# Local and down-sampled attention feeding a feed-forward layer on one core: leaner softmax steps for the first two batches, one long pass over the last eight weight chunks, and wide idle products tied to the chain

## The chip, the core and the metric

The kernel runs on one core of one Trainium2 chip. The core has a matrix engine (PE, whose weight loads are listed as PEld), a vector engine (DVE), a scalar engine (ACT), a GpSimd engine (POOL) and a queue engine (SP) that issues most of the transfers. Each engine takes its instructions strictly in the order in which the program was written for it and waits on semaphores for the others. The metric is device time in microseconds (us) of a whole execution, lower is better.

## The reference, cut to what matters

There are 8 batches, 8 heads, 576 positions and a head width of 64. Each head's attention is the sum of two softmax attentions; all heads side by side then form the rows of a feed-forward layer.

```python
q_d = q.reshape(B, H, Sd, factor, D).mean(axis=3)      # factor 4, Sd = 144; k_d, v_d likewise
out_d = sm_attn(q_d, k_d, v_d)                         # full softmax over 144 positions
out_up = np.repeat(out_d, factor, axis=2)
mask = np.abs(pos[:, None] - pos[None, :]) < factor    # band of 7 positions
scores = np.where(mask, scale * (q @ k.T), -1e9)
out_local = softmax(scores) @ v
x = (out_up + out_local)                               # -> 4608 rows of 512
h = x @ w_in                                           # 512 x 2048
g = h * np.cos(h)
return g @ w_out                                       # 2048 x 512
```

## The kernel before, in words

**Attention units.** A unit is a pair of heads of one batch, four to a batch. Its steps are `u_qk` (load q and k, add each four neighbouring columns: line 490 on DVE, or lines 483 and 485 on POOL), `u_v` (load v twice: `vdn` for the down-sampled part, `vl` for the band), `u_s` (products of scores on PE, the softmax on DVE, ACT and POOL), `u_t` (transpose the probabilities, line 632 on DVE and line 648 on PE) and `u_pv` (probabilities by values on PE, lines 665 and 677, their sum on DVE at line 696, and the split of the result into x's high and low part, lines 711 and 399). Batches 0 and 1 (`b < NEARLY`) come before and between the first feed-forward steps; their tiles lie in the memory that later holds weight chunks 8 to 15, so in the profile they carry names such as `wxi` and `wxo`, and `xxl`. `sml` and `smd` are the scores of the band and of the down-sampled part, `su` the sums, `mxl` and `mxd` the maxima, `ptl` and `ptd` the transposed probabilities, `xs` the unit's output. A unit below is called (batch, pair), as in (1,0).

**Feed-forward.** The 4608 rows are 12 tiles of 384, the inner width 16 chunks of 128. One step is a tile by a chunk: `gemm1` (line 739, 12 products), then cosine work on ACT and DVE (lines 748 to 757), then two steps later `gemm2` (line 775, 9 products into three banks). Weights come as 64-bit words and are split into a high and a low part by lines 420 to 432 and 399 (`xxh` is their scratch; the input and the output matrix give two such splits for a chunk). `PASSES` sets the steps' order: tiles 0 to 2 take chunks in four groups of four, so each of these tiles is summed up in the output by four passes, each evacuated (line 791) and written; from tile 3 on one pass takes all 16 chunks.

**What sets the order.** `Plan` keeps every step as an operation with an estimated duration, and `schedule()` lays them out by list scheduling in the planner's own time; each engine's program is then written in that order. An operation with alternatives (`alts`) goes to the engine that would end it sooner. The first 40 loads are chained: each waits until the third one before it has landed (`AHEAD`), so a load's issue in the trace marks that landing. On PE, gaps of the plan are filled with wide idle products of an identity (line 892, `ident_b`, 128x512, result unused); ahead of each `u_s`, `u_t` and `u_pv` step of batch 0 stand at least two of them (`warm=2`).

## Time and profile before

| | us |
|---|---|
| median of 3 runs (lowest, highest) | 1010.02 (1004.89, 1184.49) |
| profiled execution, its time | 1007.4 |
| profiled execution, span first to last instruction | 1005.6 |
| PE busy | 981.2 (98%) |
| DVE busy | 681.7 (68%) |
| ACT busy | 610.2 (61%) |
| POOL busy | 221.3 (22%) |
| the chain that ended last: share of PE | 87% |

The span of the profiled execution is 1.8 us shorter than its time. Rows of a time line give the start, the busy time, the engine, the line and the operation, the tile written and the tiles read, the shape and the count. Busy times of neighbours overlap a little, since an instruction starts before the one ahead has wholly left the engine. The tables of windows give busy time (and count) for PE, PEld, DVE, ACT and POOL, then the granted clock of PE as a share of the full one, the share of the 16 DMA engines and GB/s.

### The profile page before, as it was taken

How to read it: one execution, taken by the hardware profiler on the slowest of the kernel's cores; microseconds unless marked ns; L12 is line 12 of the kernel's file. 1: busy time of each engine (PE TensorE's matmuls, PEld its weight loads, DVE VectorE, ACT ScalarE, POOL GpSimd, SP SyncE). 2: the span in 40 equal slices, each digit the busy share in tenths (PEclk: the TensorE clock that was granted, in tenths of full speed). 3: DMA queues.
4: the chain of work that ended last, by engine and by line, in shares of the span. 5: the costliest groups of instructions: out<-in, count | busy, mean ns of one | idle time of the engine just before them, and what ended most of it. 6: DMA issues, size and time to landing. Idle time of an engine off the chain costs nothing.

```text
span 1005.6 us, 23855 instructions
## 1 busy us (share of the span) xinstructions
PE 981.2 (98%) x9917; PEld 847.3 (84%) x9917; DVE 681.7 (68%) x1362; ACT 610.2 (61%) x1174; POOL 221.3 (22%) x280
## 2 busy tenths in 40 slices
PE   8878999999999999999999999999999999999998
PEld 4546899899887888889888888888888888899997
DVE  7799899986587578464758957655657865433433
ACT  3457588876576656555547746654646665655554
POOL 6775325631153202000002211200001300000000
PEclk9979799999999999999999999999999999999999
DMA  7784643424355322210212312201112320100000
GB/s 224 234 270 149 215 159 64 80 36 68 67 116 132 78 65 70 68 33 28 81 49 71 129 49 58 83 26 36 62 54 73 112 65 4 37 1 1 32 1 32
DMA packets 41051, 80.70 MB, mean 80 GB/s; under 512 B 4976, under 2 KB 16240, under 8 KB 40944
## 3 DMA queue, kind: packets, MB, share of 16 engines
q1 hardware_dynamic: 37056, 72.11, 23.2%
q0 software_dynamic: 3888, 7.08, 5.0%
q8 instruction: 78, 1.28, 0.5%
q14 instruction: 29, 0.24, 0.1%
HBM read 57.93 MB, written 16.52 MB: 74 GB/s over the span
## 4 chain that ended last, share of the span: by engine, by line
PE 87%; DVE 6%; DMA 4%; issue 1%; ACT 1%; SPq 0%; ACTq 0%; DVEq 0%
PE bank L775 38%; PE bank L739 38%; PE bank L539 2%; PE bank L684 2%; PE bank L555 2%; PE bank L665 2%; PE bank L648 1%; DMA q<-qT 1%; DMA wdi<-w_in 1%; PE bank L892 1%; PE bank L677 1%; DMA vl<-vl 1%; DVE su L609 1%; DMA wxi<-qT 0%; DVE wxo L615 0%
## 5 line engine op out<-in xcount | busy, mean ns | idle before, releaser
L775 PE MATMUL bank<-wo,gh 128*128 128x512 f32 x1152 | 363.5, 396 | 0.0
L775 PEld LDWEIGHTS bank<-wo,gh 128*128 128x128 f32 x1152 | 210.0, 188 | 38.0 <-issue 3.1
L775 PE MATMUL bank<-wo,gl 128*128 128x512 f32 x576 | 227.6, 396 | 0.0
L750 ACT ACTIVATE tr<-bank,bmagic 128x384 f32<-128x384 f32 x192 | 110.9, 577 | 113.5 <-PE bank L739 109.7
L754 DVE SCALAR_TENSOR_TENSOR tr<-tr,bank 128x384 f32<-128x384 f32 x192 | 105.0, 547 | 108.0 <-ACT tr L749 107.1
L751 DVE SCALAR_TENSOR_TENSOR tr<-tr,bank 128x384 f32<-128x384 f32 x192 | 105.6, 550 | 84.2 <-ACT tr L750 83.2
L748 ACT ACTIVATE tr<-tr 128x384 f32<-128x384 f32 x192 | 100.7, 524 | 77.0 <-DVE tr L751 76.4
L756 ACT ACTIVATE gh<-tr 128x384 fp32r<-128x384 f32 x163 | 85.3, 523 | 88.3 <-DVE tr L754 86.8
L399 DVE TENSOR_TENSOR gl<-tr,gh 128x384 fp32r<-128x384 f32 x154 | 92.4, 600 | 63.5 <-ACT gh L756 60.5
L775 PEld LDWEIGHTS bank<-wo,gl 128*128 128x128 f32 x576 | 108.0, 187 | 23.5
L739 PE MATMUL bank<-x0h,wi 128*128 128x384 f32 x384 | 107.5, 340 | 0.0
L739 PE MATMUL bank<-x1h,wi 128*128 128x384 f32 x384 | 107.1, 339 | 0.0
L739 PE MATMUL bank<-x2h,wi 128*128 128x384 f32 x384 | 106.8, 338 | 0.0
L739 PE MATMUL bank<-x3h,wi 128*128 128x384 f32 x384 | 106.5, 338 | 0.0
L749 ACT ACTIVATE tr<-tr 128x384 f32<-128x384 f32 x192 | 100.8, 525 | 6.1
L399 POOL TENSOR_TENSOR gl<-tr,gh 128x384 fp32r<-128x384 f32 x38 | 43.0, 1132 | 269.6 <-DVE gh L757 175.8
L739 PEld LDWEIGHTS bank<-x0h,wi 128*128 128x128 f32 x384 | 70.5, 189 | 2.6 <-issue 0.5
L739 PEld LDWEIGHTS bank<-x1h,wi 128*128 128x128 f32 x384 | 70.3, 188 | 2.6 <-issue 0.6
L739 PEld LDWEIGHTS bank<-x2h,wi 128*128 128x128 f32 x384 | 70.2, 188 | 2.3 <-issue 0.4
L739 PEld LDWEIGHTS bank<-x3h,wi 128*128 128x128 f32 x384 | 70.2, 188 | 2.0
L739 PE MATMUL bank<-x0l,wi 128*128 128x384 f32 x192 | 64.6, 337 | 0.0
L739 PE MATMUL bank<-x3l,wi 128*128 128x384 f32 x192 | 64.6, 336 | 0.0
(199 smaller groups left out, 1452.6 us busy)
## 6 DMA issues: line engine op xcount, KB each, us to landing
vl<-vl SPq DMA_DIRECT2D x26, 384.0 KB
out<-ob SPq DMA_DIRECT2D x36, 256.0 KB
wdi<-w_in SPq DMA_DIRECT2D x16, 512.0 KB
wdo<-w_out SPq DMA_DIRECT2D x16, 512.0 KB
q<-qT SPq DMA_DIRECT2D x26, 292.0 KB
k<-kT SPq DMA_DIRECT2D x26, 292.0 KB
vd<-vdn SPq DMA_DIRECT2D x26, 288.0 KB
out<-ob POOLq DMA_DIRECT2D x27, 256.0 KB, 5.2
```

Source lines behind the costliest of these rows:

```text
L399: f = lambda e: lambda: e.tensor_tensor(out=out(), in0=in0(), in1=in1(), op=ALU.subtract)
L539: pe.matmul(banks[h].get()[BS * g:BS * (g + 1), c:c + BS], q.get()[hs, o:o + BS], k.get()[hs, o:o + BS], start=True, stop=True)
L555: pe.matmul(banks[h].get()[:HD, i * SD:(i + 1) * SD], qkd.get()[hs, 0, i * HD:(i + 1) * HD], qkd.get()[hs, 1, :], start=True, stop=True)
L665: pe.matmul(banks[0].get()[64 * h:64 * h + 64, 2 * SD:3 * SD], vd.get()[:, kh, 64 * h:64 * h + 64], ptd.get()[:, h, kh, :], start=(kh == 0 ...
L739: pe.matmul(ph.get()[:, :m], w[:, i, kc, :], x[:, kc, :], start=(n == 0), stop=(n == 3 * KC - 1))
L748: act.activation(tr.get(), tr.get(), AF.Sin, scale=PI)
L749: act.activation(tr.get(), tr.get(), AF.Square)
L750: pl.op("ACT", _act(m, True, 1), lambda: act.activation(tr.get(), h(), AF.Identity, bias=bmagic), r=[ph], w=[tr])
L751: pl.op("DVE", _dve(m), lambda: dve.scalar_tensor_tensor(out=tr.get(), in0=tr.get(), scalar=MAGIC, in1=h(), op0=ALU.subtract, op1=ALU.subt ...
L754: pl.op("DVE", _dve(m), lambda: dve.scalar_tensor_tensor(out=tr.get(), in0=tr.get(), scalar=0.5, in1=h(), op0=ALU.subtract, op1=ALU.mult), ...
L756: pl.op("ACT", _act(m, False), lambda: act.activation(gh.get(), tr.get(), AF.Copy), r=[tr], w=[gh], alts=[("DVE", _dve(m / 2), lambda: dve ...
L775: pe.matmul(o, (gh, gh, gl)[k].get()[:, sl], wo.get()[:, (0, 1, 0)[k]], start=(c == c0 and k == 0), stop=(c == c1 - 1 and k == 2))
```

## The change

It has five parts, all but one confined to batches 0 and 1.

1. **Band mask on PE.** Two products of the identity with a mask in bfloat16 open each score bank, and the score products add to them. DVE then takes the row maxima straight from the bank (new line 582, 192 columns, two per unit) and subtracts them from the bank (line 584, two per unit). Before, DVE added the mask (line 569, twice), took the maxima over 384 columns (line 574), and a subtraction of 384 columns (line 399) ran on DVE or POOL.
2. **No sum of v's four phases.** The additions of lines 504 and 505 are left out; the down-sampled product runs over all 8 pieces of `vdn` instead (line 686, 16 small products per unit for 4).
3. **`smd` is scaled on ACT** (line 639) in every unit, and no longer on DVE, POOL or ACT (lines 615 and 621).
4. **Passes.** Tiles 0 to 2 take chunks 0 to 3, 4 to 7 and then 8 to 15 in one stretch: three passes for four.
5. **Wide products.** The fixed two ahead of batch 0's steps are gone (`warm=0`). A gap's products are dealt out over the predecessors of the waiting operation, at 0.8 of the time, and the first product of each portion waits for its predecessor.

```diff
-PASSES = [(t, c, c + NF) for c in range(0, NC, NF) for t in range(3)] + [(t, 0, NC) for t in range(3, NT)]
+PASSES = [(t, c, e) for c, e in ((0, NF), (NF, 2 * NF), (2 * NF, NC)) for t in range(3)] + [(t, 0, NC) for t in range(3, NT)]
...
-           fgap=0.4, f0=0.8, fend=300.0, warm=2)
+           fgap=0.4, f0=0.8, fend=300.0, warm=0, fill=0.8)
...
+        if b < NEARLY:
+            st[(b, pr)].update(vd=vd4, vl=vt)
+            return
...
         def l_mm():
+            if b < NEARLY:
+                for h in range(2):
+                    pe.matmul(banks[h].get()[:, LQ:LQ + NSEG * BS], ident_b, mask[:, h:h + NSEG].rearrange("p s n -> p (s n)"),
+                              start=True, stop=False)
...
-                                  q.get()[hs, o:o + BS], k.get()[hs, o:o + BS], start=True, stop=True)
+                                  q.get()[hs, o:o + BS], k.get()[hs, o:o + BS], start=False, stop=(n % NSEG == NSEG - 1))
...
+        if b < NEARLY:
+            for h in range(2):
+                mx = pl.buf(None)
+                using(banks[h], pl.op("DVE", _dve(NSEG * BS), lambda h=h: dve.tensor_reduce(
+                    out=segs(mxl, h), in_=lq(h), axis=AX.X, op=ALU.max), r=[loc[h]], pw=[mxl], w=[mx]))
+                using(banks[h], pl.op("DVE", _dve(NSEG * BS), lambda h=h: dve.tensor_tensor(
+                    out=segs(sml, h), in0=lq(h), in1=segs(mxl, h).unsqueeze(2).broadcast_to([P, NSEG, BS]), op=ALU.subtract),
+                    r=[loc[h], mx], pw=[sml]))
...
-                alts.append(("ACT", 4 * _act(SD, False, 1), scaled))
-            pl.op("POOL", _pool(size), f(pool), r=[su], w=[sm], alts=alts, shares=True)
+                pl.op("ACT", 4 * _act(SD, False, 2), scaled, r=[su], w=[sm])
+            else:
+                pl.op("POOL", _pool(size), f(pool), r=[su], w=[sm], alts=alts, shares=True)
...
         def d_mm():
+            if b < NEARLY:
+                for i in range(8):
+                    for h in range(2):
+                        pe.matmul(banks[0].get()[64 * h:64 * h + 64, 2 * SD:3 * SD], vd.get()[:, i, 64 * h:64 * h + 64],
+                                  ptd.get()[:, h, i // 4, :], start=(i == 0), stop=(i == 7))
+                return
...
+                    for (x, d), (y, _) in zip(marks, marks[1:] + [(o.start - 0.2, None)]):
+                        n = int((y - x) * CFG["fill"] / 0.22)
...
+                        for i in range(n):
+                            ins = pe.matmul(s[2].get(), ident_b, ident_b.unsqueeze(1).broadcast_to([P, 4, P]), start=True, stop=True)
+                            if d and not i:
+                                tc.add_manual_dep(ins.ins, made[d].ins.name, mybir.DependencyInfo(
+                                    mybir.DependencyClass.Sync, mybir.DependencyReason.DATA), reason="spread")
```

The planner lays everything out anew, so instructions move on all engines. Three places matter below.

PE around unit (0,3), the last of batch 0, before (`ident_b` rows are the wide products; `k,q` are those of unit (1,0)):

```order
L648 MATMUL bank<-ident,wxi_214 72x72 x4
L546 MATMUL bank<-k,q 32x32 x48
L892 LDWEIGHTS ident_b
L892 MATMUL bank<-ident_b 128x512
L892 LDWEIGHTS ident_b
L892 MATMUL bank<-ident_b 128x512
L648 MATMUL bank<-ident,wxi_214 72x72 x4
L892 LDWEIGHTS ident_b
L892 MATMUL bank<-ident_b 128x512
L892 LDWEIGHTS ident_b
L892 MATMUL bank<-ident_b 128x512
L677 MATMUL bank<-wxi_560,wxo_585 64x24 x48
```

The same place after the change:

```order
L668 MATMUL bank<-ident,wxi_211 72x72 x4
L538 LDWEIGHTS ident_b
L538 MATMUL bank<-mask,ident_b 128x192
L538 LDWEIGHTS ident_b
L538 MATMUL bank<-mask,ident_b 128x192
L553 MATMUL bank<-k,q 32x32 x48
L668 MATMUL bank<-ident,wxi_211 72x72 x4
L703 MATMUL bank<-wxi_555,wxo_589 64x24 x48
L686 MATMUL bank<-wxo_274,wxi_579 64x144 x16
L562 MATMUL bank<-qkd 72x144 x4
```

The wide products between the steps are gone, the two mask products are new, and the down-sampled product has 16 instructions. The scores of unit (1,0) still stand between the two transposes of unit (0,3).

DVE from the outputs of batch 0's last units to the softmax of unit (1,0), before (`wxo_480` and `wxi_568` are the outputs of units (0,2) and (0,3)):

```order
L696 TENSOR_TENSOR wxo_480<-bank,wxo_390 128x3x96 x2
L423 TENSOR_SCALAR xxh<-xxh 128x512 x2
L425 SCALAR_TENSOR_TENSOR xxh<-wdi_385,xxh 128x512
L425 SCALAR_TENSOR_TENSOR xxh<-wdo_449,xxh 128x512
L696 TENSOR_TENSOR wxi_568<-bank,wxi_560 128x3x96
L427 SCALAR_TENSOR_TENSOR xxh<-wdi_385,xxh 128x512
L427 SCALAR_TENSOR_TENSOR xxh<-wdo_449,xxh 128x512
L696 TENSOR_TENSOR wxi_568<-bank,wxi_560 128x3x96
L399 TENSOR_TENSOR wi_946<-xxh,wi_946 128x512
L399 TENSOR_TENSOR wo_951<-xxh,wo_951 128x512
L399 TENSOR_TENSOR x0l<-wxi_568,x0h 128x384
L399 TENSOR_TENSOR x1l<-wxi_568,x1h 128x192
```

The softmax of unit (1,0) begins only behind these rows. After the change (`wxo_490` and `wxi_579` are those outputs now):

```order
L490 TENSOR_REDUCE qkd<-k 128x144
L425 SCALAR_TENSOR_TENSOR xxh<-wdo_459,xxh 128x512
L722 TENSOR_TENSOR wxo_490<-bank,wxo_402 128x3x96 x2
L427 SCALAR_TENSOR_TENSOR xxh<-wdo_459,xxh 128x512
L399 TENSOR_TENSOR x0l<-wxo_490,x0h 128x384
L490 TENSOR_REDUCE qkd<-q 128x144
L399 TENSOR_TENSOR wo_954<-xxh,wo_954 128x512
L582 TENSOR_REDUCE mxl<-bank 128x6 x2
L584 TENSOR_TENSOR sml<-bank,mxl 128x192 x2
L490 TENSOR_REDUCE wxo_205<-wxo_820 128x144
L722 TENSOR_TENSOR wxi_579<-bank,wxi_555 128x3x96 x2
L599 TENSOR_REDUCE mxd<-bank 72x2
```

The sums over q and k of unit (1,0) have moved from POOL to DVE, and the unit's maxima now stand ahead of the last output of batch 0.

DVE behind the transpose of unit (1,0) to the softmax of unit (1,1), before:

```order
L427 SCALAR_TENSOR_TENSOR xxh<-wdi_656,xxh 128x512
L569 TENSOR_TENSOR wxi_276<-bank,mask 128x192 x2
L582 TENSOR_REDUCE mxd<-bank 72x2
L574 TENSOR_REDUCE mxl<-wxi_276 128x12
L582 TENSOR_REDUCE mxd<-bank 72x2
L399 TENSOR_TENSOR wxi_276<-wxi_276,mxl 128x384
L423 TENSOR_SCALAR xxh<-xxh 128x512
```

And after:

```order
L427 SCALAR_TENSOR_TENSOR xxh<-wdi_603,xxh 128x512
L423 TENSOR_SCALAR xxh<-xxh 128x512
L425 SCALAR_TENSOR_TENSOR xxh<-wdo_695,xxh 128x512
L399 TENSOR_TENSOR wi_1148<-xxh,wi_1148 128x512
L582 TENSOR_REDUCE mxl<-bank 128x6 x2
L584 TENSOR_TENSOR wxi_300<-bank,mxl 128x192 x2
L599 TENSOR_REDUCE mxd<-bank 72x2 x2
L777 SCALAR_TENSOR_TENSOR tr<-tr,bank 128x384
```

The softmax has shorter instructions, and more of the weights' split (lines 423 to 427 and 399) stands among them.

56 lines of the change are left out of this document (38 added, 18 removed).

## The prediction

> **What bounds the kernel now.** I read the page first, then the matrix engine's windows, then whom it waits for, then the time lines and groups of the first 110 us. Tile 1's first feed-forward product starts at 110.47 us, and that point cuts the run in two:
>
> ```profile
> 0.00:47.61 47.61, 41.28 (x1042) 24.06 (x1042) 35.58 (x75) 19.45 (x67) 32.45 (x66) 0.96 0.77 233
> 47.61:110.47 62.86, 51.77 (x984) 36.34 (x983) 58.75 (x111) 38.58 (x98) 37.03 (x42) 0.84 0.63 201
> 110.47:1005.60 895.13, 888.17 (x7896) 786.86 (x7894) 587.34 (x1178) 552.20 (x1010) 151.80 (x173) 1.00 0.24 64
> ```
>
> From 110.47 on PE is busy 888.17 of 895.13 us at full clock. Ahead of it PE is busy too, but much of that is wide products without use, and the granted clock is 0.96 and then 0.84. Behind 110.47 little can be won unless PE's work shrinks; of its waits from 120 us on, two matter:
>
> ```profile
> PE bank L684 <- DMA ptb<-sml: 1.5, 3, 0.9
> PE bank L648 <- DVE smd L615: 0.8, 1, 0.8
> ```
>
> The change removes nothing of PE's work behind that point: in the order of instructions tile 1's first product has all eight early units and the same four `gemm1` and two `gemm2` steps of tile 0 ahead of it in both kernels, and behind it come the same products and two wide ones more. **So the question is when that product starts (T0)**, and what then disturbs a full PE. DVE's transposes of batch 1 cut the time before T0:
>
> ```profile
> L632 DVE STREAM_TRANSPOSE wxi<-wxi x2: 558/559/560, 73.7 to 101.4; 128x384 f32<-128x384 f32 x2
> L632 DVE STREAM_TRANSPOSE sml<-sml x1: 565/565/565, 59.1 to 59.1; 128x384 f32<-128x384 f32 x1
> L632 DVE STREAM_TRANSPOSE wxo<-wxo x1: 560/560/560, 87.9 to 87.9; 128x384 f32<-128x384 f32 x1
> ```
>
> Stretch A ends with the transpose of unit (1,0) at 59.1 (`sml`), stretch B with that of (1,3) at 101.4, 42.3 us for three units; stretch C, 9.1 us, ends at T0. In B, DVE is hardly idle (58.75 busy of 62.86 us above), but some of its time is stall. These are the products by the sums between 58 and 104 us, and the maxima and subtractions of the first 110 (shortest, median and longest in ns):
>
> ```profile
> L615 DVE TENSOR_TENSOR wxi<-wxi,su x3: 541/734/1373, 71.1 to 100.6; 72x576 f32<-72x576 f32 x2, 128x384 f32<-128x384 f32 x1
> ...
> L615 DVE TENSOR_TENSOR wxo<-wxo,su x1: 2806/2806/2806, 84.8 to 84.8; 72x576 f32<-72x576 f32 x1
> ```
>
> ```profile
> L574 DVE TENSOR_REDUCE mxl<-wxi x4: 534/538/540, 10.7 to 92.1; 128x12 f32<-128x384 f32 x4
> L399 DVE TENSOR_TENSOR wxi<-wxi,mxl x4: 542/689/1642, 11.6 to 92.9; 128x384 f32<-128x384 f32 x4
> ```
>
> The maxima never vary; the subtraction takes 0.54 or 1.64 us, the product 0.73 or 2.81. POOL was busy for 37.03 us of that window.
>
> **Stretch A: the first unit of batch 1 comes sooner.** Its k must land first. The first 40 loads are chained by threes, so the issue at 34.84 marks k's landing, and the two behind it, in the same way, that of the unit's two pieces of v:
>
> ```profile
> 34.84 0.33 SPq L476 DMA_DIRECT2D wxo<-qT  x1
> ...
> 50.90 0.34 SPq L498 DMA_DIRECT2D wxo<-vl  x1
> 52.16 0.32 SPq L497 DMA_DIRECT2D wxo<-vdn  x1
> ```
>
> The change keeps the order of the first 39 loads, so 34.84 stays. In the new order DVE's first instruction that needs it is the sum over k; 27 more stand between that and the transpose of unit (1,0). Prices, over the first 110 us:
>
> ```profile
> L421 DVE TENSOR_SCALAR xxh<-xxh x11: 353/414/1220, 33.0 to 107.9; 128x512 f32<-128x512 f32 x11
> L423 DVE TENSOR_SCALAR xxh<-xxh x11: 401/520/1490, 37.2 to 109.7; 128x512 int32<-128x512 int32 x11
> L425 DVE SCALAR_TENSOR_TENSOR xxh<-wdi,xxh x5: 676/764/1074, 38.4 to 107.3; 128x512 int32<-128x512 int32 x5
> L425 DVE SCALAR_TENSOR_TENSOR xxh<-wdo,xxh x5: 677/678/1219, 39.4 to 104.3; 128x512 int32<-128x512 int32 x5
> L427 DVE SCALAR_TENSOR_TENSOR xxh<-wdi,xxh x5: 622/676/845, 44.6 to 109.1; 128x512 int32<-128x512 int32 x5
> ```
>
> ```profile
> L582 DVE TENSOR_REDUCE mxd<-bank 72x2 f32<-72x288 f32 x16 | 7.0, 440 | 0.0
> ...
> L569 DVE TENSOR_TENSOR wxi<-bank,mask 128x192 f32<-128x192 f32 x8 | 2.4, 340 | 1.4 <-PE bank L555 1.4
> ...
> L490 DVE TENSOR_REDUCE wxo<-wxo 128x144 f32<-128x576 f32 x2 | 1.5, 739 | 0.0
> ```
>
> By medians: three sums over q and k at 0.74, 2.2; the weights' split (three of line 421, two of 423, two of 425, one of 427, one subtraction like it) 5.2; four output sums and two maxima, 288 columns from a bank like line 582, at 0.44, 2.6; three passes over 384 columns at 0.54, 1.6; two instructions on 16 columns at no more than 0.34, 0.7. The new maximum over 192 columns from a bank is in no row: it lies between line 569 (192 columns from a bank, 0.34) and line 582 (288, 0.44). I take 0.34, the same width, for it, for the new subtraction and for one cast, five in all, 1.7. Sum 14.0, and 34.84 + 14.0 = 48.8. Overlap of neighbours could give 1 us back, stalls could cost 4. **A ends at 50 (48 to 53) instead of 59.1.** What goes is an order: before, unit (1,0)'s softmax stood behind all of batch 0's outputs. PE keeps up, as the products show:
>
> ```profile
> 27.64 0.71 PE L665 MATMUL bank<-wxo 72*64 72x144 f32 x8
> 28.29 1.68 PE L892 MATMUL bank<-ident_b 128*128 128x512 bf16 x7
> ...
> 34.52 1.59 PE L677 MATMUL bank<-wxo,wxi 32*64 32x24 f32 x96
> ...
> 100.44 1.03 PE L648 MATMUL bank<-ident,wxi 72*72 72x72 f32 x8 [1.68 <-DVE wxi L615]
> ...
> 103.41 2.77 PE L677 MATMUL bank<-wxi,wxo 32*64 32x24 f32 x96
> ```
>
> The long product of unit (0,3) has 32 rows where 8 took 0.65 us (27.64 to 28.29): 2.6 us, 2.0 more than before, at half clock up to twice that. With the band's product (1.6) and the scores of (1,0) behind 34.84 it ends near 41, and DVE's order reaches that output at about 42. Where it were later, DVE would wait and A with it.
>
> **Stretch B: DVE has other work, not less.** Counted in the order between the same two transposes, this goes: six mask additions 2.0, three maxima 1.6, three subtractions (1.64, and two at 0.54) 2.7, three products (0.73, 1.37, 2.81) 4.9; 11.2. This comes: twelve 192-column instructions, 4.1. And the planner has slid in one more of line 421, two of 423, two of 425, one of 427, one weight subtraction and one sum over q (5.1), and eight others at a 384-column price (4.3). B would be 42.3 - 11.2 + 4.1 + 9.4 = 44.6. But medians do not hold what stalls remain in 42.3, and POOL loses the sums of v and most of those over q and k. The other end is PE's own work between these points, with the steps of a full PE as price:
>
> ```profile
> 140.20 2.10 PE bank L739 x12
> 142.31 2.08 PE bank L775 x9
> ```
>
> 34 wide products at 0.24 (seven from 28.29 on) 8.2, three band products 4.8, three long ones 7.8, three `gemm1` 6.3, two `gemm2` 4.2: 31.3, and with scores and transposes, which I put at 5, some 36. **I take 41, nearer to DVE's end (36 to 46).** The Trainium skill, in "SBUF — State Buffer", section "Who interferes with whom", says that a reduction never contends with GpSimd, nor a vector instruction with one SBUF input outside the two-port modes, while one with two does. By that rule the excess of the removed rows (1.1 and 2.1 us) would go for good and B would be nearer 38. The trace agrees as far as line 574 never varies and line 399 does.
>
> **Stretch C.** Behind the last transpose come the band's product, the long one, batch 2's first scores, and x's low part. Before, this ran at half clock: 2.77 us at 103.41 for the product that takes 1.59 at 34.52. A warm clock gives some 3 us back, the long product takes 2: I keep **9 (7 to 11)**. A wide product queued ahead of a step now waits for a predecessor of that step and can hold it up by its portion, 14 of them or 3.3 us at most; B's range has room for it.
>
> **The rest.** Mask products and ACT's scaling lie beside DVE's sums (ACT is busy 38.58 of 62.86 us). Nine evacuations and nine accumulating writes less spare ACT, DVE and POOL, which PE hardly waits for behind T0: nothing. The long stretch wants chunks 12 to 15 eight steps sooner; in the order, the last DVE product of chunk 15's input half stands behind step 23's cosine work, and step 31 is the first to need it, so eight steps at 2.10 + 2.08, 33 us, cover it. Tile 0 is free for batch 2 at step 32 instead of 40, which may end part of the two waits above (2.3 us): 1.1 off, and 0.5 on for two wide products.
>
> **Sum.** T0 = 50 + 41 + 9 = 100, 10.5 sooner; with the 0.6, 11.1. The profiled execution took 1007.4 us, 1.8 above its span: **996 us**. Before's median is 1010.02 and its lowest run 1004.89; the profiled one lies between, so I add nothing.
>
> **Rivals.**
> - *Given back (0.20).* A's lead is real, but B turns into a chain that alternates between two full engines, each softmax queued behind slid-in splits: B 46 or more, T0 105 to 110, 1001 to 1006 us. For it: 44.6 by plain prices. Against: two stalls of 3.2 us go.
> - *More (0.12).* No stall and a warm clock: T0 = 48 + 36 + 7 = 91, and both waits go: 1007.4 - 19.5 - 2.3 = 985.6.
> - *Cold PE, the slower one (0.05).* Without its fixed wide products batch 1 could stay at half clock, to which PE falls easily:
>
> ```profile
> 54.00:56.00 2.00, 0.00 (x0) 0.00 (x0) 2.00 (x5) 0.09 (x1) 1.92 (x2) 1.00 0.85 206
> 64.00:66.00 2.00, 2.00 (x6) 1.08 (x5) 2.00 (x2) 0.92 (x4) 2.00 (x2) 0.50 0.93 286
> ```
>
> At 54 it idles, and at 64 it still runs at 0.50 though full. At 103.41 it was cold again after no longer idling than the 1.68 us at 100.44. Were all of B cold, PE's 36 would be 72, C 13 and T0 135: 1031 us. It decides once the clock stays at 0.50 for most of B; for half of it, PE's 54 would make 1014. Against: portions dealt out over the predecessors cut the gaps up. The Trainium skill, "TensorE: Matmul & The Clock Gate", section "What's actually happening", has the clock halve after an idle window of some 3.4 us. By that rule cut-up gaps would never get there and this rival would be out; the row at 100.44 speaks against the rule, so the rival keeps a chance.
> - *Late weights (0.03).* DVE falls over 33 us behind by step 28 and PE waits in the long stretch; 10 us beyond that cost the whole lead, 1006 us.
>
> The forecast keeps 0.60. The range takes A, B and C near their ends (T0 91 to 110) and a little of the cold case: 985 to 1009. Two per cent, about what a measurement of this kernel can tell from no change, is 20 us: faster 0.12, within 0.83, slower 0.05.
>
> **What would show it.** Tile 1's first `gemm1` product near 100 us; the transposes of (1,0) and (1,3) near 50 and 91; line 686's 32 rows in 2.6 us; 192-column rows near 0.34; PE's waits from 120 us on at 2 us or less; PE's busy time behind T0 near 888. I am wrong in A if DVE waits for something other than k between 35 and 50 us, in B if three units take over 46 us, in C if the clock reads 0.50 there, and altogether if PE waits between steps 24 and 32.

## The result, and the profile after

The changed kernel takes **1015.0 us** (median of 12 runs, 1010.5 to 1020.2) against 1005.0 of the kernel before (12 runs beside it): ratio 1.0093, with 95 per cent between 1.0072 and 1.0114. It is slower by 0.9 per cent; the forecast was 996, so it went the other way and out of the range. One run of the kernel before took 1184.49 us, far from its other eleven, and is not in the ratio.

The same cut as in the prediction, at the first `gemm1` product of tile 0 and of tile 1, from the windows of the changed kernel (the columns are as there: the stretch, its length, PE, weight loads, DVE, ACT, POOL, then the granted clock):

```profile
0.00:62.24 62.24, 55.84 (x1118) 41.68 (x1118) 34.96 (x87) 23.99 (x80) 18.14 (x48) 0.70 0.70 208
62.24:117.05 54.81, 52.18 (x1087) 38.28 (x1085) 52.91 (x114) 40.63 (x109) 26.41 (x27) 0.97 0.67 228
117.05:1018.40 901.35, 892.02 (x7898) 789.28 (x7896) 585.27 (x1164) 546.28 (x1001) 142.15 (x163) 1.00 0.21 59
```

T0 is **117.05** where 100 was forecast and 110.47 stood before. The first stretch now has a granted clock of 0.70 (before: 0.96). The transposes of batch 1, which bound stretches A and B (groups by tile, first and last start at the end):

```profile
L652 DVE STREAM_TRANSPOSE wxi<-wxi x2: 560/561/562, 78.2 to 107.1; 128x384 f32<-128x384 f32 x2
L652 DVE STREAM_TRANSPOSE sml<-sml x1: 565/565/565, 67.3 to 67.3; 128x384 f32<-128x384 f32 x1
```

So A ends at 67.3 (forecast 50), B lasts 39.8 (41), C 10.0 (9). Where A went, the matrix engine's time line shows:

```profile
20.56 0.56 PE L703 MATMUL bank<-sml,vl 32*64 32x24 f32 x15
23.36 2.34 PE L703 MATMUL bank<-sml,vl 32*64 32x24 f32 x81 [2.24 <-issue]
25.63 4.11 PE L686 MATMUL bank<-ptd,vd 72*64 72x144 f32 x32
...
49.30 1.51 PE L553 MATMUL bank<-k,q 64*32 64x32 f32 x96
...
51.36 2.77 PE L703 MATMUL bank<-wxi,wxo 32*64 32x24 f32 x96
54.06 4.11 PE L686 MATMUL bank<-wxo,wxi 72*64 72x144 f32 x32
58.10 1.24 PE L562 MATMUL bank<-qkd 64*72 64x144 f32 x8
59.27 3.32 PE L940 MATMUL bank<-ident_b 128*128 128x512 bf16 x9
```

From 23.36 to 59.27 it has no gap, and all of it runs at half clock: the long product (line 686, 32 instructions; the first and the last of four are shown) takes 4.11 us each time, and the band's product (line 703, 96 instructions) 2.77. Windows of the same kernel say it in one row, 36 us of 36 busy at 0.50:

```profile
24.00:60.00 36.00, 36.00 (x619) 30.35 (x616) 15.57 (x35) 11.46 (x33) 9.27 (x15) 0.50 0.68 201
```

DVE is busy for 15.57 of these 36 us. Its time line around the sum over k of unit (1,0) and behind it shows the longest waits. An output of batch 0 (line 722) waits for ACT's copy of a long product's result, and ACT itself waits 3.25 and 5.41 us for line 686 ahead of the two copies:

```profile
39.24 0.82 DVE L722 TENSOR_TENSOR wxi<-bank,wxi 128x288 f32<-128x288 f32 x2 [2.99 <-ACT wxi L465]
...
42.25 0.74 DVE L490 TENSOR_REDUCE qkd<-k 128x144 f32<-128x576 f32 x1
...
48.79 0.82 DVE L722 TENSOR_TENSOR wxo<-bank,wxo 128x288 f32<-128x288 f32 x2 [4.63 <-ACT wxo L465]
...
59.41 0.36 DVE L584 TENSOR_TENSOR sml<-bank,mxl 128x192 f32<-128x192 f32 x1 [5.25 <-PE bank L562]
...
60.34 0.81 DVE L722 TENSOR_TENSOR wxi<-bank,wxi 128x288 f32<-128x288 f32 x2
```

The wait of 5.25 us is for the second half of the scores of unit (1,0) (line 562); of the unit's maxima and subtractions over 192 columns only the last subtraction stands behind it. From 42.25 to the transpose at 67.30 DVE waits for 11.1 us and is busy for 13.9.

Behind T0 the profiled execution lost 6.2 us more (901.35 us against 895.13). These are its waits from 120 us on:

```profile
PE bank L765 <- DVE tr L780: 2.2, 3, 1.0
PE bank L710 <- DMA ptb<-sml: 1.9, 2, 1.6
PE bank L668 <- DVE smd L633: 0.7, 1, 0.7
```

The first is new. The second and third existed before, but one of the second is now 1.6 us long. Two stretches behind T0 are cold. The first follows a wait of the third kind and one of the first (0.74 and 0.99 us between 261.9 and 264.4), and PE is full in it (five-microsecond windows):

```profile
260.00:265.00 5.00, 3.27 (x21) 2.43 (x20) 4.08 (x10) 2.21 (x5) 1.45 (x2) 1.00 0.00 2
265.00:270.00 5.00, 5.00 (x23) 4.32 (x22) 2.45 (x5) 2.93 (x7) 0.00 (x0) 0.66 0.16 39
```

The second follows the wait of 1.6 us, which ends at 346.1. Most of this part seems to belong to this one execution, the longest of the twelve (1020.2 us): seven kernels below have the same order of work behind T0 (1, 6, 8, 12, 13, 15, 16), and in their profiles the time behind T0 is 896.1 to 896.8 us. With 896.7 in place of 901.35 and the 1.8 us around the span, 117.05 makes 1015.5, within 0.6 us of the median. The 1.6 us left behind T0 can't be told from none, since the three kernels with the order of the kernel before differ by more there (893.9 to 898.2: before, 2, 14). **What has to be explained is T0.**

### The profile page after: what moved, and what is told of

Read it like the earlier page. It is cut to its first block, busy times and chain, and to the rows that moved or that the text cites. A ratio compares the mean times of both kernels' runs of the same rounds, so it can differ in the third digit from the quotient of the medians.

```text
span 1018.4 us, 24152 instructions
## 1 busy us (share of the span) xinstructions
PE 1000.0 (98%) x10097; PEld 869.3 (85%) x10097; DVE 673.1 (66%) x1363; ACT 610.9 (60%) x1187; POOL 186.7 (18%) x236
## 4 chain that ended last, share of the span: by engine, by line
PE 80%; DVE 3%; DMA 2%; ACT 1%; issue 0%; SPq 0%; ACTq 0%; DVEq 0%
PE bank L801 36%; PE bank L765 36%; PE bank L546 2%; PE bank L710 2%; PE bank L562 1%; PE bank L691 1%; PE bank L668 1%; DMA ptb<-sml 1%; DMA k<-kT 1%; DVE tr L780 0%; DVE gl L399 0%; DVE xxh L427 0%; DVE xxh L423 0%; DVE smd L633 0%; DVE su L627 0%
## 5 line engine op out<-in xcount | busy, mean ns | idle before, releaser
L782 ACT ACTIVATE gh<-tr 128x384 fp32r<-128x384 f32 x155 | 81.2, 524 | 87.6 <-DVE tr L780 86.1
L765 PE MATMUL bank<-x0h,wi 128*128 128x384 f32 x384 | 107.2, 339 | 0.5 <-DVE tr L780 0.4
L765 PE MATMUL bank<-x1l,wi 128*128 128x384 f32 x192 | 64.9, 338 | 0.0
L765 PE MATMUL bank<-x2l,wi 128*128 128x384 f32 x192 | 64.5, 336 | 0.0
```

The costliest lines, as they stand in the source:

```text
L765: pe.matmul(ph.get()[:, :m], w[:, i, kc, :], x[:, kc, :], start=(n == 0), stop=(n == 3 * KC - 1))
L782: pl.op("ACT", _act(m, False), lambda: act.activation(gh.get(), tr.get(), AF.Copy), r=[tr], w=[gh], alts=[("DVE", _dve(m / 2), lambda: dve ...
```

## The experiments

Theory after the comparison: with no fixed wide products, batch 0 runs at half clock, and the long product, four times in PE's queue, makes PE the bound of A. Rivals: the length of PE's queue alone; the order on DVE; the long stretch (for the loss behind T0); program blocks that arrive late. The cuts (in us) come from one profile each, the medians from 4 to 12 runs (16: one), beside which the kernel before had medians of 1003.9 to 1005.8. So a difference of two medians of separate rows can be off by some 2 us; the ratios compare runs made side by side. Executions of one kernel lie up to 15 us apart (8: 1007.4 to 1022.4), so where cut and median differ, the median decides.

| kernel | A ends | T0 | behind T0 | median | ratio to before, 95% |
|---|---|---|---|---|---|
| before | 59.1 | 110.5 | 895.1 | 1005.0 | |
| changed | 67.3 | 117.05 | 901.4 | 1015.0 | 1.0072 to 1.0114 |
| 1 fixed products back | 62.2 | 113.9 | 896.7 | 1009.6 | 1.0018 to 1.0055 |
| 2 before, none fixed | 59.8 | 108.6 | 898.2 | 1004.9 | 0.9973 to 1.0014 |
| 3 two stretches | 62.0 | 111.8 | 902.8 | 1015.9 | 1.0063 to 1.0152 |
| 4 = 1 and 3 | 58.8 | 110.8 | 901.1 | 1016.2 | 1.0079 to 1.0136 |
| 5 = 1, v summed | 62.8 | 111.9 | 896.3 | 1005.7 | 0.9988 to 1.0030 |
| 6 one burst | 62.0 | 112.5 | 896.1 | 1010.4 | 1.0030 to 1.0089 |
| 7 = 1, mask on DVE | 59.3 | 107.2 | 896.2 | 1005.7 | 0.9990 to 1.0039 |
| 8 = 1, old wide rule | 59.1 | 110.1 | 896.2 | 1013.0 | 1.0046 to 1.0119 |
| 9 = 5 and 7 | 57.3 | 108.8 | 899.8 | 1010.1 | 1.0008 to 1.0059 |
| 10 before, long stretch | 59.9 | 111.2 | 896.5 | 1007.4 | 0.9989 to 1.0045 |
| 11 = 9, two stretches | 58.6 | 107.9 | 902.6 | 1009.0 | 1.0001 to 1.0056 |
| 12 = 1, no other wide | 58.2 | 111.0 | 896.6 | 1014.1 | 1.0040 to 1.0102 |
| 13 two loads in flight | 63.1 | 116.2 | 896.8 | 1015.1 | 1.0061 to 1.0128 |
| 14 before, two in flight | 64.2 | 119.5 | 893.9 | 1015.8 | 1.0076 to 1.0143 |
| 15 = 1, two in flight | 59.2 | 121.4 | 896.6 | 1020.1 | 1.0085 to 1.0202 |
| 16 narrow burst | 69.2 | 119.0 | 896.7 | 1017.5 (one run) | |
| 17 = 9, none fixed | 55.0 | 110.4 | 895.0 | 1009.2 | 1.0013 to 1.0057 |
| 18 v summed, none fixed | 57.5 | 110.6 | 895.3 | 1008.8 | 1.0014 to 1.0060 |

### The clock of batch 0 (1, 2, 6, 16)

**1.** Edit:

```diff
-           fgap=0.4, f0=0.8, fend=300.0, warm=0, fill=0.8)
+           fgap=0.4, f0=0.8, fend=300.0, warm=2, fill=0.8)
```

> Edit: the changed kernel with two wide products fixed ahead of each of batch 0's steps again (warm=2); nothing else. Theory (cold batch 0: with hardly any wide product, the matrix engine's clock falls at the first wait near 21 us and the small products alone never raise it): clock 1.00 from 24 us to the end of batch 0, the 32 rows of line 686 in about 2.2 us instead of 4.1, transpose of unit (1,0) near 50 to 54 instead of 67.3, tile 1's first gemm1 product near 100 to 104 instead of 117.05, 901 us behind it as before this edit, time about 1000 us (998 to 1004). Rival (the order and the longer product make A late, whatever the clock): the 32 extra wide products only add work, tile 1's first product stays at 115 to 120, time 1015 to 1020.

Measured: 1009.6 us, 5.4 less than the changed kernel; full clock in batch 0 but for 0.79 between 36 and 44 us; T0 113.9. This is between the theory and its rival: the clock came back as expected, a long product takes 2.18 us again, yet A still ends at 62.2, not near 52. PE's queue at full clock, from the time line:

```profile
47.14 1.05 PE L553 MATMUL bank<-k,q 64*32 64x32 f32 x96
...
49.34 1.59 PE L703 MATMUL bank<-wxi,wxo 32*64 32x24 f32 x96
...
51.41 2.18 PE L686 MATMUL bank<-wxo,wxi 72*64 72x144 f32 x32
53.52 0.71 PE L562 MATMUL bank<-qkd 64*72 64x144 f32 x8
```

The first half of the scores of unit (1,0) (line 553) ends at 48.2, the second (line 562) at 54.2, behind the band's and the long product of unit (0,3), and DVE waits for it (2.59 us at 54.30). The first sum over k starts at 42.21, as without the fixed products (42.25); behind it DVE waits for 6.1 us instead of 11.1. So the clock is 5.1 us of A, and what remains of A's loss stands at full clock too.

**2.** Edit: `warm=2` to `warm=0` in the kernel before.

> Edit: the kernel before with no wide product fixed ahead of batch 0's steps (warm=0); those that it put into planned gaps stay. Theory (cold batch 0): the clock stands at 0.50 over a good part of 24 to 48 us, line 677's 96 rows cost 2.8 us instead of 1.6, tile 1's first product starts 2 to 12 us later than 110.47, time 1006 to 1017 against 1005 of the kernel before. Rival (the fixed products don't hold the clock): within 2 us of the kernel before or faster, 1002 to 1006.

Measured: 1004.9 us, no difference, although the clock was 0.60 from 16 to 32 and 0.51 from 36 to 48 us, and line 677 took 2.77 us there. The rival's time, by another reason than it gave: the clock did fall, and A (59.8) didn't mind.

**6.** Edit:

```diff
-                    least = CFG["warm"] if ahead else 0
+                    least = 12 if o.name == "u_t" and o.arg == (0, 2) and not burst else 0
+                    burst += [1] * (least > 0)
...
-    made = {}
+    made, burst = {}, []
```

> Edit: the changed kernel, with no fixed products, but with one burst of 12 wide products (2.6 us at full clock, 5.2 at half) ahead of the transposes of unit (0,2). Theory (small products don't raise the clock, wide ones do, and small ones hold it while nothing stalls): 0.50 from the first stall near 20 us to that burst near 35 us, 1.00 behind it until the next stall of 1 us or more; the transpose of (1,0) at 60 to 65 instead of 67.3, tile 1's first gemm1 at 110 to 115, time 1009 to 1014. Rival (the clock comes back by the mere passing of time, or falls again with the first small products): 0.50 up to the nine wide products at the end of batch 0, or 1.00 well ahead of the burst, time 1014 or more.

**16.** Edit, on top of 6:

```diff
+                            if least:
+                                ins = pe.matmul(s[2].get()[:64], ident_b[:72, :64], ident_b[:72].unsqueeze(1).broadcast_to([72, 4, P]), start=True, stop=True)
+                            else:
+                                ins = pe.matmul(s[2].get(), ident_b, ident_b.unsqueeze(1).broadcast_to([P, 4, P]), start=True, stop=True)
```

> Edit: the sixth experiment with its burst of 12 products made of 72 rows and 64 columns of the same constant, each still 512 columns long, in place of 128 rows and columns. If it is the short products' overhead that leaves the clock at half, this burst restores it as the wide one did (about 3 us after its start) and the groups behind it run at full clock; if it is the part of the array in use, the clock stays at 0.50 through it and up to the nine wide products at the end of batch 0. By the rows at hand I take the second: line 686's groups of 32 products ran 4.1 us back to back at half clock without any rise.

Measured: 6 took 1010.4 us, 4.6 less than the changed kernel; 16 took 1017.5. The time lines around the two bursts and the windows behind them, first 6, with its burst of 128 rows and columns:

```profile
35.62 5.03 PE L941 MATMUL bank<-ident_b 128*128 128x512 bf16 x12
40.49 0.41 PE L668 MATMUL bank<-ident,wxo 72*72 72x72 f32 x4
...
43.47 2.18 PE L686 MATMUL bank<-wxi,wxo 72*64 72x144 f32 x32
```

```profile
36.00:40.00 4.00, 4.00 (x11) 1.50 (x10) 1.42 (x3) 0.02 (x1) 0.00 (x0) 0.50 0.85 264
40.00:48.00 8.00, 7.55 (x249) 6.03 (x247) 5.16 (x9) 5.11 (x13) 4.95 (x6) 0.98 0.84 263
48.00:52.00 4.00, 3.93 (x124) 3.93 (x126) 3.02 (x6) 0.76 (x2) 3.73 (x7) 0.81 0.57 173
```

And 16, whose burst has as many products of the same length, on 72 rows and 64 columns:

```profile
35.46 5.33 PE L942 MATMUL bank<-ident_b 72*64 72x512 bf16 x12
40.72 0.69 PE L668 MATMUL bank<-ident,wxo 72*72 72x72 f32 x4
...
46.23 4.11 PE L686 MATMUL bank<-wxi,wxo 72*64 72x144 f32 x32
```

```profile
36.00:40.00 4.00, 4.00 (x11) 1.66 (x10) 1.42 (x3) 0.01 (x1) 0.00 (x0) 0.50 0.65 193
40.00:48.00 8.00, 8.00 (x126) 5.95 (x126) 3.63 (x5) 3.12 (x7) 3.99 (x5) 0.50 0.84 243
48.00:52.00 4.00, 4.00 (x84) 3.28 (x84) 1.29 (x3) 1.29 (x4) 0.80 (x2) 0.50 0.60 176
```

The wide burst restored the clock by its end, the narrow one didn't, and PE was full in both. In 6 the clock then held over six microseconds of small products (from 41.95 us, behind four more wide ones), and fell again at 50 to 51 us, 3 us after the start of a pause of 0.52 us at 47.55. So the small products didn't raise the clock, and by these two runs that is a matter of the rows and columns of the array that they use, not of their length. That the pause made it fall is likely, not shown: a pause of 1.35 us at 16.78 in the changed kernel didn't.

### Which part of PE's queue (5, 7, 9, 17, 18)

**5.** Edit, on top of 1 (the two additions over v, and `vd`, stand as in the kernel before):

```diff
-        if b < NEARLY:
-            st[(b, pr)].update(vd=vd4, vl=vt)
-            return
...
-            if b < NEARLY:
-                for i in range(8):
...
-            pl.op("PE", 2.1, d_mm, r=[vd, ptd], pw=[banks[0]], w=[poo])
+            pl.op("PE", 0.64, d_mm, r=[vd, ptd], pw=[banks[0]], w=[poo])
```

> Edit: as the first experiment (two fixed wide products ahead of each of batch 0's steps), and v is again summed over its four parts ahead of the product for batches 0 and 1, so that the product has 8 rows in place of 32. Theory (batch 0 is bound by the matrix engine's own queue, of which the long product is 2.18 us a unit against 0.65): the product of the first scores of (1,0) moves up by about 4 x 1.5 = 6 us from 53.5, the transpose of (1,0) from 62.2 to 55 to 58, tile 1's first gemm1 from 113.9 to 102 to 108, time 1000 to 1005 us. Rival (A is bound by DVE or by the loads, the long product lies beside them): the transpose stays at 60 or later, time 1008 to 1012.

Measured: 1005.7 us, 3.9 less than 1. The first half of the scores moved from 47.14 to 41.85, as reckoned, but the second half only from 53.5 to 50.6 (this execution was partly cold from 24 to 36 us: 0.80, 0.50, 0.85), and the planner then put unit (1,0)'s maxima behind batch 0's outputs; A ended at 62.8. The time came near the theory's range (1000 to 1005), the profile's A as its rival had it: with one execution this isn't decided by 5 alone.

**7.** Edit, on top of 1: DVE's additions of the mask (now in float32), its one maximum and one subtraction over 384 columns as in the kernel before, and

```diff
-            if b < NEARLY:
-                for h in range(2):
-                    pe.matmul(banks[h].get()[:, LQ:LQ + NSEG * BS], ident_b, mask[:, h:h + NSEG].rearrange("p s n -> p (s n)"),
-                              start=True, stop=False)
...
-                                  q.get()[hs, o:o + BS], k.get()[hs, o:o + BS], start=False, stop=(n % NSEG == NSEG - 1))
+                                  q.get()[hs, o:o + BS], k.get()[hs, o:o + BS], start=True, stop=True)
```

> Edit: as the first experiment (fixed wide products back), and the mask is again added by DVE (two additions, one maximum over 384, one subtraction over 384) in place of a product into the bank and four instructions over 192 columns. Theory (before tile 1's first gemm1 both PE and DVE are full, and DVE's saving per unit is 4.5 us against 0.8 of PE): B grows from 39.8 to 42 to 46 us, tile 1's first gemm1 from 113.9 to 115 to 120, time 1011 to 1016. Rival (PE alone binds): B shrinks by 3 x 0.8 us and the time falls to 1006 to 1009.

Measured: 1005.7 us, 3.9 less than 1; T0 107.2; B 38.4 us, shorter than 39.8. The time is on the rival's side (PE alone binds), its reason is not. These are the windows of B in four profiles, in this order 1, 7, 12 (no wide product in B) and 9:

```profile
62.20:101.97 39.77, 37.73 (x811) 28.22 (x809) 38.22 (x89) 30.54 (x80) 17.52 (x17) 1.00 0.60 193
59.29:97.71 38.42, 37.10 (x809) 28.39 (x796) 37.55 (x86) 29.90 (x79) 16.97 (x20) 1.00 0.68 218
58.19:98.84 40.65, 32.01 (x779) 26.86 (x779) 38.29 (x88) 30.64 (x80) 17.49 (x17) 0.92 0.58 189
57.31:100.31 43.00, 38.87 (x769) 26.51 (x768) 41.04 (x83) 33.15 (x82) 26.76 (x27) 1.00 0.61 209
```

DVE fills B in all of them (38.22 of 39.77 us in 1, 37.55 of 38.42 in 7), and in 12 PE has 8.6 us to spare without B being shorter. B didn't grow in 7 since the new plan has less other work in it: the sums of one unit's v, a sum over q and two casts are gone from it (2.5 us), and the weights' split takes 18.8 us instead of 20.3. With v summed on DVE and POOL as well, the mask's work on DVE does lengthen B: 43.0 in 9 against 40.1 in 5, and 45.0 in 17 against 40.6 in 18.

**9.** Edit: 5 and 7 together. **17.** The same with `warm=0`.

> Edit: the fifth and the seventh experiment together: v summed ahead of the product and the mask added by DVE as in the kernel before, two fixed wide products as before; what is left of the change is the long stretch, the wide products that follow the chain, and ACT's scaling without a choice. Theory (the matrix engine's queue binds everything ahead of tile 1's first gemm1, so what the smaller elementwise work put on it is a loss): the two gains add, that product at 103 to 108 against 113.9 with both in place, time 1000 to 1004, below the kernel before. Rival (once PE is relieved, DVE binds again with its 4.5 us a unit): product at 109 or later, time 1005 to 1009.

> Edit: the ninth experiment (v summed ahead, mask added by DVE) without the fixed wide products. Theory (half clock costs only where the matrix engine's queue is the bound of stretch A, which the long product and the mask's product made it): with both taken off, the cold batch 0 is hidden by DVE as in the second experiment; transpose of unit (1,0) within 3 us of the ninth's 57.3, time within 3 us of its 1010.1. Rival (half clock always costs): transpose at 62 or later, time 1013 to 1018.

Measured: 9 took 1010.1 us, not 1000 to 1004. A ended at 57.3 (59.3 in 7), but B at 43.0 (38.4 in 7) gave more than that back, as the rival had it (DVE binds again), and T0 is 108.8; behind T0 stood 899.8 us with a wait of 2.0 us for batch 2's `ptb`, and the median agrees with the profile. The gains of 5 and 7 don't add: B's length is one reason, the part behind T0 is not explained. 17 took 1009.2, within 3 us of 9 as the theory had it: 0.50 from 24 to 32 us cost nothing there, and A ended at 55.0. 9 holds nothing of the change's first two parts, and 11 below nothing of the fourth either, yet both stay 4 to 5 us above the kernel before. What is left in 11 are the new rule for wide products and ACT's scaling of `smd` in all units of batches 0 and 1. 8 takes the rule back on top of 1 and gains nothing; the scaling was taken back in no run by itself, so what it costs stays open.

**18.** Edit: 5's on the changed kernel itself (`warm=0`).

> Edit: the changed kernel with v summed ahead of the product (8 rows in place of 32) and nothing else; no fixed products. Theory (the long product at half clock, 4.11 us against 1.23, four times, is what made stretch A 17 us longer than forecast): A shortens by 4 x 2.9 us or until DVE binds, transpose of unit (1,0) at 57 to 62 instead of 67.3, tile 1's first gemm1 at 106 to 112 instead of 117, time 1005 to 1010. Rival (the clock alone, whatever the product): transpose at 64 or later, time 1012 or more.

Measured: 1008.8 us, 6.2 less than the changed kernel by this one edit; A 57.5 and T0 110.6, all in the theory's ranges. PE's time line of 18 (line 559 is the second half of the scores, 694 the band's product):

```profile
23.81 0.71 PE L682 MATMUL bank<-ptd,vd 72*64 72x144 f32 x8
...
40.77 0.84 PE L694 MATMUL bank<-wxi,wxo 32*64 32x24 f32 x19 [2.12 <-issue]
...
44.52 1.24 PE L559 MATMUL bank<-qkd 64*72 64x144 f32 x8
```

The second half of the scores starts at 44.52 instead of 58.10. But the clock is no longer 0.50 throughout batch 0 (it is full from 16 to 36 us, and 0.50 from 40 to 44), and the new plan has more wide products between the steps. So 18 shows what the long product cost with all that follows from it; how much of that is the product's own length and how much the clock, it doesn't separate. What binds A has changed, too. The windows from 34.84 us, the landing of k that the prediction started from, to the end of A, in this order for the changed kernel, 1 and 18:

```profile
34.84:67.30 32.46, 32.22 (x452) 24.94 (x453) 18.34 (x39) 12.35 (x36) 14.48 (x20) 0.60 0.55 161
34.84:62.20 27.36, 25.44 (x464) 17.28 (x461) 18.48 (x39) 12.37 (x36) 14.50 (x20) 0.94 0.68 198
34.84:57.49 22.65, 19.43 (x335) 11.68 (x336) 19.54 (x34) 9.54 (x28) 17.63 (x23) 0.85 0.80 243
```

DVE has as much to do in each (18.3 to 19.5 us), and is idle for 14.1, 8.9 and 3.1. In 18 A is nearly DVE's own work. Two stops without a cause, 2.1 us at 40.77 and 2.9 us at line 543 ahead of T0, are still in it.

### The long stretch (3, 4, 10, 11)

**3.** Edit:

```diff
-PASSES = [(t, c, e) for c, e in ((0, NF), (NF, 2 * NF), (2 * NF, NC)) for t in range(3)] + [(t, 0, NC) for t in range(3, NT)]
+PASSES = [(t, c, c + NF) for c in range(0, NC, NF) for t in range(3)] + [(t, 0, NC) for t in range(3, NT)]
```

**4.** 1 and 3. **10.** The reverse of 3 on the kernel before. **11.** 9 and 3.

> Edit: the changed kernel with chunks 8 to 15 in two stretches of four again for tiles 0 to 2. Theory (the long stretch packs DVE's work into 117 to 207 us and so makes the new waits and clock dips behind tile 1's first product): that product stays near 117 us, the time behind it falls from 901 to 895 or 896, time 1009 to 1011 us. Rival (the 6 us behind it come from the early phase ending late, not from the stretches): 901 stays, time 1014 to 1016.

> Edit: both edits at once, fixed wide products back and chunks 8 to 15 in two stretches; what is left of the change is the smaller elementwise work and the wide products that follow the chain. If the cold batch 0 (15 us) and the long stretch (6 us) are what the change lost, and they add: tile 1's first product near 100 to 104, 895 behind it, time 994 us (991 to 998), below the kernel before by about 1 per cent. If the smaller elementwise work itself is what costs: 1005 or more.

> Edit: the kernel before with chunks 8 to 15 at one stretch for tiles 0 to 2; nothing else. Theory (the four kernels with the long stretch that kept its order all show a wait of gemm1 for the cosine of 2.2 to 2.5 us behind 117, which the kernel before doesn't have): that wait appears, nothing moves ahead of 100 us, tile 1's first gemm1 within 3 us of 110.5, time 1004 to 1008. Rival (the wait comes from the later start of the early phase): no such wait, time 1002 to 1005.

> Edit: the ninth experiment with chunks 8 to 15 in two stretches; of the change only the wide products that follow the chain and ACT's scaling are left. Theory: tile 1's first gemm1 at 103 to 108 as in the ninth, and behind it either the kernel before's 895 us, time 1000 to 1003, or the wait for x3h and x3l (2.6 us) that the third and fourth showed, with its cold stretch, 899 to 901 and time 1004 to 1008, which would put that wait on the stretches and the new wide rule, not on the elementwise work.

Measured: 3 and 4 refute the theory that the long stretch made the loss behind T0. With two stretches the time behind it is 902.8, 901.1 and 902.6 us (3, 4, 11), longer than the 896.1 to 896.8 of the seven like kernels and the 899.8 of 9; in 3 and 4 `gemm1` waits 2.0 and 2.2 us for `x3h`, in 11 2.7 us for the cosine, and a cold stretch follows. On the kernel before, the long stretch does what 10's theory said and no more (waits behind 125 us):

```profile
PE bank L739 <- DVE tr L754: 1.5, 3, 1.0
PE bank L684 <- DMA ptb<-sml: 0.4, 2, 0.2
```

The wait for the cosine is new. The 1.4 us that stand behind T0 beyond the kernel before (896.5 against 895.1) are less than before, 2 and 14 differ by there, and the time, 1007.4, can't be told from 1005.0.

### The wide products elsewhere (8, 12)

**8.** Edit, on top of 1: the portions and `add_manual_dep` of the changed kernel give way to the rule of the kernel before (`n = int((o.start - s[0] - CFG["fgap"]) / 0.43)` or `/ 0.3`). **12.** Edit, on top of 1: `fill=0.8` to `fill=0.0`.

> Edit: as the first experiment, but the wide products are dealt out by the rule of the kernel before: one portion for each planned gap, at most two fixed, bound to no predecessor; the rest of the change stays. Theory (the clock in batch 0 comes from the fixed ones, and the ones that follow the chain are neither gain nor loss): tile 1's first gemm1 within 3 us of 113.9, time 1007 to 1012. Rival (the ones that follow the chain hold real products up): tile 1's first gemm1 at 108 to 110, time 1003 to 1006. Rival the other way (without them batch 1 cools): clock 0.50 in parts of 65 to 105 us, that product at 117 or later, time 1013 or more.

> Edit: as the first experiment (fixed products in batch 0), but no wide product anywhere else behind the start (portions of zero). Theory (small products don't restore the clock, gemm1 and gemm2 do): batch 1's stretch from 60 to 105 us keeps its clock mostly through the gemm1 and gemm2 steps between the units, with 0.50 for 5 to 15 us in all; 34 wide products at 0.24, 8 us, leave a full PE; tile 1's first gemm1 between 108 and 116, time 1004 to 1012. Rival of the prediction (batch 1 cold without them): 0.50 for most of 65 to 105, that product at 125 or later, time 1020 or more.

Measured: 1013.0 and 1014.1 us, 3.4 and 4.5 more than 1. The profiled execution of each was among its fastest (T0 110.1 and 111.0), so where the medians lost it isn't shown. By the times, the wide products behind batch 0, and their following the chain, are a small gain; for 8 the intervals (1.0046 to 1.0119, against 1.0018 to 1.0055) overlap a little. In 12 the clock was 0.50 from 52 to 60 and from 96 to 112 us, not over most of batch 1: the rival of the prediction, a batch 1 that goes cold as a whole, did not come even without these products.

### The stops without a cause (13, 14, 15)

Ahead of 117 us PE stops in the middle of groups, and waits for nothing that the profile shows: 1.20, 1.35 and 2.24 us in the changed kernel, after 447, 694 and 951 of its instructions (products and weight loads counted). In five other kernels (before, 1, 2, 3, 4) they come after 445 or 446, 694 to 697, 951, 1206, 1457 to 1461, 1707, 1962 to 1967, 2721 to 2732, 3738, 3999 and 4255 to 4257, and only twice elsewhere: at multiples of 256, if the records lack the 65 to 102 instructions that are missing to the next multiple. That they do is inferred, not shown. The view of the DMA queues shows what fits that, 16 packets of 0.26 MB in all, 16 KB each, in a queue named for instructions (0 to 117 us):

```profile
q1 hardware_dynamic: 13356, 25.07, 67.5%
q8 instruction: 16, 0.26, 0.9%
```

The other queue, with the loads, moves a hundred times as much. The Trainium skill, "Runtime: NRT & Kernel Launch", section "Instruction fetch mechanics", has blocks of 256 instructions fetched ahead, at a cost mostly hidden; the block size agrees with the counts, and if the stops are these blocks, the cost isn't always hidden here ahead of 117 us.

**13, 14, 15.** Edit, on the changed kernel, the kernel before, and 1:

```diff
-AHEAD, FIRST = 3, 40
+AHEAD, FIRST = 2, 40
```

> Edit: the changed kernel with its first 40 loads chained by twos in place of threes; nothing else. Theory (the stops come from program blocks that queue behind the loads): the stops sum to 1.5 to 3 us ahead of 60 us instead of 4.8, the one at 21 us shrinks below 1 us, the clock then holds longer, the transpose of unit (1,0) at 55 to 65 instead of 67.3, time 1005 to 1013 unless the loads themselves get later by more than 3 us. Rival (the stops have nothing to do with the loads' depth): they stay at 4 us or more and at 0.50 from the second or third of them, time 1013 to 1018.

> Edit: the kernel before with its first 40 loads chained by twos. It is the control: its stops sum to 2.2 us and cost little, since its wide products restore the clock; if two in flight only delays the loads, tile 1's first gemm1 is 1 to 5 us later than 110.5 and the time 1006 to 1010; if it relieves the program blocks without delaying the loads, 1003 to 1005.

> Edit: the first experiment (changed kernel with two fixed wide products ahead of each of batch 0's steps) with its loads chained by twos. Theory: its stops shrink from 5.4 to 2 to 3 us, tile 1's first gemm1 from 113.9 to 109 to 112, time 1005 to 1008. Rival (loads later by as much): 1009 to 1013.

Measured: the stops of the changed kernel sank from 4.8 to 1.2 us and those of 1 from 5.0 to 2.8, those of the kernel before stayed (2.2 and 2.1). But all three are no faster, 14 and 15 some 11 us slower than with three in flight, since the loads come later (the thirtieth is issued at 53.3 and 51.2 us instead of 42.5 and 41.5). And 13 shows that the clock is lost without the stop at 21 us, too, behind another pause at the same place (its time line and windows):

```profile
21.02 1.76 PE L703 MATMUL bank<-sml,vl 32*64 32x24 f32 x92 [1.01 <-DVE ptd L466]
```

```profile
20.00:21.00 1.00, 0.01 (x2) 0.00 (x0) 1.00 (x4) 1.00 (x5) 0.00 (x0) 1.00 0.62 184
...
24.00:56.00 32.00, 32.00 (x540) 26.27 (x535) 15.52 (x36) 11.75 (x35) 8.86 (x15) 0.50 0.69 205
```

One microsecond's wait for DVE, three microseconds of small products at full clock, and then 32 us full at 0.50.

## Why the prediction was wrong, point by point

- **What bounds the kernel, and T0 as the question: held.** Of the 10 us between the medians, 6.6 lie ahead of T0 by the two profiles and at most some 1.6 behind it by the seven like profiles; the profiled execution of the kernel before was itself 2.4 above its median.
- **Stretch A, 50 forecast, 67.3 measured: the step that failed.** The sum of DVE's chain held: 14.0 us reckoned, 13.9 busy (though it counts three sums over q and k where the order has four). Two other things in it failed.
  - *The chain starts when k lands, at 34.84.* By the same mark k landed at 33.20, but from 34.84 on DVE's order has 4.4 us of work of batch 0 and of the split ahead of that sum, and a wait of 3.0 us in it. The sum started at 42.25, 7.4 us late, and at full clock as late (42.21 in 1).
  - *"PE keeps up".* It didn't: DVE waited for another 11.1 us inside the chain. The prediction had the long product of unit (0,3) end near 41 and DVE reach its output at about 42; they came at 58.2 and 60.3. It counted the long product once, 2.0 us more, where PE's queue holds four of them (5 moved the scores up by 5.3 us). It left out that the second half of the scores of (1,0) stands behind unit (0,3)'s long product. And it used prices at full clock.

  The 7.4 and the 11.1 us make up the whole distance from 48.8. The sign I had named came true: between 35 and 59 us DVE waited for PE and ACT, not for k. Of the 11.1, 5.1 are the clock (1); by medians, the clock of batch 0 was worth 5.4 (1) and 4.6 (6). No kernel reached 50: with the long product gone, too, A is 57.5 (18) and 55.0 (17).
- **The clock alone is no loss, the longer queue is.** Half clock cost nothing where the queue was short (2 against the kernel before, 17 against 9); DVE is busy there for 19.5 of 24.9 us (2) and 16.9 of 20.2 (17) from 34.84 to the end of A, so most of A is its own work there. At full clock the long product was worth 3.9 us by the medians (1 against 5; the intervals overlap a little), and so was the mask's product (1 against 7), but not both together (9). At the changed kernel's clock the long product, with all that follows from it, was worth 6.2 us (18).
- **Stretch B, 41 forecast, 39.8 measured: right, near DVE's end as I had placed it, with that end priced too high.** DVE is busy for 38.2 of the 39.8 us where plain prices made 44.6. DVE's saving counts in B where the plan doesn't fill it with other work: 2.9 and 4.4 us (9 against 5, 17 against 18). By the rule from the Trainium skill, "SBUF — State Buffer", section "Who interferes with whom", I had 38. The rows over 192 columns from a bank never stalled (0.29 to 0.36 us, 32 of them), but 39.8 lies between 38 and 41 and decides nothing.
- **Stretch C, 9 forecast, 10.0 measured:** inside its range, with some luck. It was not warm throughout, as the clock of 0.97 over the second stretch hides (0.60 in 112 to 116 us), and in the seven like kernels C lies between 9.8 and 12.3 us.
- **"The rest", 0.6 gained forecast:** 6.2 lost in the profiled execution, some 1.6 in seven others, which is within what like kernels differ by. The term left out that the long stretch brings a wait of its own, for the cosine (2.2 us, and 1.5 in 10), and that such waits can be followed by half clock (265.4 to 268.8 and 347.3 to 350.7 us).
- **Prices:** the instructions over 192 columns took 0.34 to 0.35, as taken. The long product took 2.18 warm, 2.6 was taken, and 4.11 cold.
- **Rivals.** The cold PE came, in batch 0, where I hadn't looked, and at a chance of 0.05. Against it I had put that cut-up gaps keep PE warm; the row I quoted myself (64 to 66 us: full, 0.50) said the opposite. The Trainium skill's rule, "TensorE: Matmul & The Clock Gate", section "What's actually happening", has the clock fall after an idle window of some 3.4 us and come back after a busy one. These runs agree with neither half for the small products: the clock fell behind pauses of 0.52 to 2.24 us, and 36 us of a PE busy mostly with small products didn't bring it back. Late weights: no such wait was seen.

No kernel here beats the one before. 5 and 7 come level with it. The parts of the change that were shown to cost are what it put on PE's queue, the long product above all, and on top of it the missing fixed products; what 9 and 11 still lose stays open.

## What to carry to other kernels

Work moved off an idle-looking engine onto the matrix engine is priced over its whole queue, each copy of it, at the clock that will be granted there: first find out whether that engine's in-order queue then ends last. A chain on an in-order engine starts when the engine gets there, not when its data land: count what stands ahead of it. A matrix engine that is busy with small products is not a warm one. Pairs of full-size products ahead of each step mostly kept the clock up (1), and twelve in a row brought it back (6); three and four in a row (1.49 and 1.91 us in the changed kernel) did not. Where the queue isn't the bound, don't bother. When two medians differ by one per cent, don't explain a single profile's last 5 us before similar kernels have shown which part of it repeats.

## What the runs showed of the hardware

- Products of 72 rows and 64 columns, 512 long, left the granted clock at 0.50 through 5.33 us back to back; as many of 128 and 128 raised it (5.03 us). Small products, with runs of three and four 512-long products of 128 and 128 among them, ran full at 0.50 for 32 to 36 us without any rise (13, the changed kernel).
- With small products the clock fell some 2 to 4 us after the start of pauses of 0.52, 1.0 and 2.24 us (6, 13, the changed kernel); a pause of 1.35 us in the changed kernel left it at 1.00.
- The clock changes in steps of 3.41 us: in all twenty profiles each stretch at one clock between two changes ahead of 125 us lasts a whole multiple of that (in the changed kernel 37.55 us at 0.50 from 23.01 on, then 51.20 at 1.00, then 3.41 at 0.50). A short pause can so cost several microseconds of half clock.
- The matrix engine can stop for 0.3 to 2.9 us at counts that fit multiples of 256 of its instructions, though not at each (three times in the first 117 us of the changed kernel). That was seen ahead of 125 us, most with the DMA engines' share at 0.76 to 0.81 over the first 50 us (three loads in flight), fewer at 0.63 to 0.67 (two), and not behind 125 us.
